# Attention by one batch at a time, two neighbouring chunks in step, with two tokens to a partition

## The chip, the cores and the metric

The kernel runs on one core of a Trainium2 chip. The core has a tensor engine (PE, with its weight loads shown apart as PEld), a vector engine (DVE), a scalar engine (ACT), GpSimd (POOL), a queue engine (SP) that issues most transfers, and 16 DMA engines that carry them. The metric is the device time of one execution in microseconds (us), as the median of the runs.

## The reference

Two blocks follow each other. The first is a causal linear attention with a decay per head, for 4 batches, 8 heads, 768 tokens and head width 64:

```
intra = (q_b k_b^T * Dmask) v_b          # Dmask[i, j] = lam^(i-j) for i >= j, else 0
inter = (q_b * lam^(i+1)) kv_state
out   = intra + inter
kv_state = lam^block * kv_state + (k_b * lam^(block-1-j))^T v_b
```

Its result, x of 4 x 768 x 512, goes into a Fourier mixing block with an MLP:

```
u  = x + real(fft(fft(x, over tokens), over channels))
un = (u - mean(u)) / sqrt(var(u) + 1e-6)
y  = u + relu(un @ w_ch1) @ w_ch2        # 512 -> 2048 -> 512
```

q, k, v are fp32; the two weight matrices arrive as 64-bit floats and are converted on the chip.

## The kernel before

**Attention.** The recurrence may be cut into chunks of any length; the kernel uses chunks of C = 128 tokens, so NC = 6 a batch. `attention` (L476 on) walks through 12 steps. A step handles the same chunk of two batches: batches 0 and 1 for the first six steps, 2 and 3 for the last six. `Side` (L309) holds the buffers of one of the two; the second side borrows room in the second halves of w1 and w2, which therefore can't be loaded before attention ends. For each side a step has these parts:

- `load`: k, q and v of a chunk, 128 tokens on 128 partitions, 256 KB each, in runs of the 64 floats that one head has for one token (L331, issued by SP, one step ahead).
- `turn_k`, `turn_q`: four transposes each on PE (L349, L357), read out of PSUM by ACT (L351, L359). POOL makes kd, k times its decay (L347). DVE makes qs, q times its decay (L363).
- `scores`: k times q for each head, 64 rows by 128 columns of the array (L370). DVE multiplies the result by the decay mask (L376).
- `from_state`: qs times the running state, 64 rows by 64 columns (L385), into the output bank po.
- `to_state`: kd times v, 128 rows by 64 columns (L392). POOL scales the old state (L398) and DVE adds (L399).
- `within`: v times the masked scores, 128 rows by 64 columns (L403), on top of po. ACT copies po out (L407).
- `back`: four transposes to tokens on partitions (L416), read out by ACT (L423 to L427), and, for batches 1 to 3, stored to DRAM. Batch 0 is kept on the chip with a mirrored copy.

In PE's order a step is scores, from_state, to_state, within, then the turns of the next step, then back.

**What follows attention.** `fft_ln(b)` folds a batch on DVE (`fold_x`, L541 to L545, and the lines after L609), transforms it by products with cosine and sine tables (L662, L674 to L679), normalises it and turns the result for the MLP (L693 to L727). `mlp` multiplies by w1 (L808) and w2 (L822). Its first three groups are done in halves of the hidden width, so that the first half can run before the second half of the weights is on the chip. Everything after that (from L900 on) is a Strassen-like scheme for the later groups, which the change doesn't touch.

**Weights.** `load_weights` (L202) brings a 512 KB piece of 64-bit floats (L215) and turns it into fp32 with two ACT and five DVE instructions (L226 to L236). There are 32 pieces. The first 16 use four raw buffers of the pool hp, the last 16 those of the pool ld that attention's loads used.

**Order.** Each of these is a generator that yields a cost; `mixed` (L1430) interleaves several by their shares of the cost. A scheduler then orders each engine's instructions by priority and hands out buffers as they come free; `keep_in_program_order` and `lead` pin some of them. The shares that matter stand at L1442 to L1458: five attention steps with a sixth of the weights; then attention with `fft_ln(0)` (`mix`); then the first half of the MLP (`lead_half`) with what is left of attention and of the first 16 pieces; then `lead_half` with `fft_ln(1)`, `fft_ln(2)` (`fr`) and the second 16 pieces. PSUM has eight banks: five in the pool pa, three in pm. While the flag `early` is set, attention takes from both; later pm is the MLP's and attention has pa alone.

Of the kernel before, what the change touches and what calls it, by code (L numbers as in the profile page):

```python
# [77 lines left out]
def kernel(  # L78
# [44 lines left out]
    ld = front_pool("ld", 2)  # L123
# [35 lines left out]
    decay = const.tile([C, H, C], F32, name="decay")  # L159
    for h in range(H):  # L160
        scan(decay[:, h, :], lamb[:, h:h + 1].broadcast_to([C, C]), ident, 0.0, op0=ALU.mult, op1=ALU.add)
# [8 lines left out]
    kpow = decay[:, :, C - 1:C].broadcast_to([C, H, D])  # L170
# [6 lines left out]
    turns_a = [const.tile([128, HP, D], F32, name=n) for n in ("st", "sd")]  # L177
# [24 lines left out]
    def load_weights(dst, src):  # L202
# [5 lines left out]
        if landed[0] < NW // 2:  # L208
            raw = hp_.tile([128, 2 * WP], U32, tag="hr", name=f"raw{cnt[0]}")
        else:  # L210
            raw = ld.tile([128, 3 * WP], U32, tag="kqv", name=f"raw{cnt[0]}")[:, 0:2 * WP]
# [72 lines left out]
    def pair(t, hp):  # L284
        return t[:, 2 * hp:2 * hp + 2, :].rearrange("p a d -> p (a d)")

    oTs, eo = {}, {}
    TWOS = ((0, 1), (2, 3))
    TURNED = (0,)
    first = const.tile([128, HP, 1], F32, name="first")  # L290

    spare = [w2[:, FO // 2 + i, :] for i in range(FO // 2)]
    spare += [w1[:, c, DFF // 2 + DM * i:DFF // 2 + DM * (i + 1)] for c in range(KO) for i in range(2)]
    turns_b = [spare[0][:, i * HP * D:(i + 1) * HP * D].rearrange("p (h d) -> p h d", h=HP) for i in range(2)]
    place = {n: spare[1 + i] for i, n in enumerate(
        ("k0", "k1", "q0", "q1", "v0", "v1", "kd", "kT", "qT", "qs", "oT", "sc0", "sc1"))}
# [11 lines left out]

    class Side:  # L309

        def __init__(self, b):
            self.b, self.two = b, b % 2
            self.turns = turns_b if self.two else turns_a
            self.kqv, self.now, self.next = {}, {}, {}

        def tile(self, shape, name, i=None):
            if self.two:
                t = place[name if i is None else f"{name}{i % 2}"]
                return t.rearrange("p (h d) -> p h d", h=shape[1])
            return new(at, shape, name, **({"bufs": 2} if name == "sc" else {}))  # L320

        def load(self, c):
            rows = slice(c * C, (c + 1) * C)
            if self.two:
                ts = [self.tile([C, H, D], n, c) for n in "kqv"]
            else:
                t = new(ld, [C, 3, H, D], "kqv")
                ts = [t[:, i] for i in range(3)]
            self.kqv[c] = ts
            for t, src in zip(ts, (k, q, v)):  # L330
                nc.sync.dma_start(t, src[self.b, :, rows, :].rearrange("h p d -> p h d"))  # L331
                yield 0.0

    sides = [Side(b) for b in range(B)]

    def lead(products):

        for i, mm in enumerate(products):
            if i == 0:
                tc.keep_in_program_order(mm)  # L340

    def turn_k(s, c):
        kt, qt, vt = s.kqv[c]
        s.next = n = {"vt": vt}
        if c < NC - 1:
            n["kd"] = s.tile([C, H, D], "kd")
            nc.gpsimd.tensor_tensor(n["kd"], kt, kpow, op=ALU.mult)  # L347
        pt = psum_t([128, HP, C])
        lead(nc.tensor.transpose(pt[:, hp, :], pair(kt, hp), ident) for hp in range(HP))  # L349
        n["kT"] = s.tile([128, HP, C], "kT")  # L350
        nc.scalar.copy(n["kT"], pt)  # L351
# [1057 lines left out]
    def run(gen):  # L1409
        return sum(gen)  # L1410
# [98 lines left out]
```

## Time and profile before

| | us |
|---|---|
| median of 3 runs | 775.61 (775.11 to 776.37) |
| the profiled execution | 773.71 |
| its span, first to last instruction | 771.9 |
| PE busy / PEld / DVE / ACT / POOL | 736.4 / 638.5 / 606.0 / 222.1 / 176.8 |
| mean granted PE clock | 0.992 of full speed |
| bytes moved | 123.36 MB in 156,651 packets, 114,478 of them under 512 B |

A profile's page gives busy times and shares, the span in 40 slices of 19.3 us (digits are tenths), the DMA queues, the chain of work that ended last, and the costliest groups of instructions. A group's line has the source line, engine, operation, output and input tiles, shapes and count, then its busy time, the mean of one in ns, and the idle time before it with what ended that. PE's instructions overlap, so a row's duration there is a latency; the distance between starts is the price. The time outside the span is 1.8 us.

### The profile page before, as it was taken

What the parts mean: (1) busy time and instruction counts of PE and PEld (TensorE: products, weight loads), DVE (VectorE), ACT (ScalarE), POOL (GpSimd) and SP (SyncE); (2) the same over time, 40 slices, a digit from 0 to 9 for tenths busy, and PEclk for the clock granted to TensorE, in tenths of its full rate; (3) what the DMA queues carried; (4) which work ended last, traced back from release to release, by engine and by line L of the source; (5) the groups of instructions that cost most, each with busy time, mean ns of one, the idle gap of its engine ahead of it and who ended that gap; (6) DMA issues with size and microseconds to landing.
All of it is one profiled execution on the core that took longest, in us unless ns stands there. A gap on an engine that the chain in (4) does not pass through costs nothing.

```text
span 771.9 us, 14917 instructions
## 1 busy us (share of the span) xinstructions
PE 736.4 (95%) x5784; PEld 638.5 (83%) x5784; DVE 606.0 (78%) x1167; ACT 222.1 (29%) x512; POOL 176.8 (23%) x200
## 2 busy tenths in 40 slices
PE   6898798998999999999899999999999999999997
PEld 5787697866586676759647899999999999999997
DVE  5988968778967488357965999788986699758984
ACT  4665444644341111002001221034301341024310
POOL 4422232210001124101105951360015001230013
PEclk9999998999999999999999999999999999999999
DMA  9999995455333346511441465876546455455542
GB/s 195 237 244 241 261 231 167 147 182 188 111 128 83 78 151 179 131 68 59 86 102 68 151 219 160 277 233 200 183 124 177 127 180 186 126 176 180 145 141 69
DMA packets 156651, 123.36 MB, mean 160 GB/s; under 512 B 114478, under 2 KB 117166, under 8 KB 156582
## 3 DMA queue, kind: packets, MB, share of 16 engines
q1 hardware_dynamic: 149232, 103.13, 48.9%
q0 software_dynamic: 4032, 12.99, 4.7%
q10 hardware_dynamic: 3318, 6.30, 2.3%
q8 instruction: 46, 0.75, 0.4%
q14 instruction: 23, 0.19, 0.1%
HBM read 90.66 MB, written 31.73 MB: 159 GB/s over the span
## 4 chain that ended last, share of the span: by engine, by line
PE 66%; DVE 14%; DMA 9%; issue 4%; SPq 3%; ACT 2%; POOL 1%; ACTq 0%; DVEq 0%; POOLq 0%
PE p L1257 19%; PE p L1183 17%; PE pm L808 8%; PE pm L822 7%; PE p L1090 6%; DMA raw<-in_moe_w_ch_dram 5%; PE pa L662 4%; SPq L331 3%; DMA w<-in_q_dram 2%; DVE w L236 1%; PE pa L370 1%; DMA ur<-utd 1%; DVE e L227 1%; ACT e L229 1%; DVE w L233 1%
## 5 line engine op out<-in xcount | busy, mean ns | idle before, releaser
L808 PE MATMUL pm<-ut,w 128*128 128x256 f32 x512 | 116.9, 381 | 5.9 <-ACT hr L816 3.3
L808 PEld LDWEIGHTS pm<-ut,w 128*128 128x128 f32 x512 | 95.5, 190 | 23.7 <-ACT hr L816 4.5
L822 PE MATMUL pm<-w,hr 128*128 128x512 f32 x240 | 104.9, 593 | 0.0
L822 PEld LDWEIGHTS pm<-w,hr 128*128 128x128 f32 x240 | 45.2, 190 | 52.6 <-issue 51.6
L1278 POOL TENSOR_TENSOR y<-y,u 128x512 f32<-128x512 f32 x12 | 19.9, 1661 | 186.8 <-DVE y L1287 100.4
L1257 PE MATMUL p<-tx,sx 128*128 128x128 f32 x400 | 52.7, 275 | 0.0
L1257 PEld LDWEIGHTS p<-tx,sx 128*128 128x128 f32 x400 | 48.6, 192 | 0.0
L1192 DVE TENSOR_TENSOR ha<-p,ha 128x512 f32<-128x512 f32 x60 | 40.0, 683 | 8.3 <-PE p L1183 8.1
L816 ACT ACTIVATE hr<-pm 128x256 f32<-128x256 f32 x44 | 16.6, 381 | 92.2 <-PE pm L808 91.8
L1263 ACT COPY y<-p 128x128 f32<-128x128 f32 x48 | 12.8, 266 | 103.6 <-PE p L1257 103.1
L1265 DVE TENSOR_TENSOR y<-p,y 128x128 f32<-128x128 f32 x92 | 25.4, 283 | 15.9 <-PE p L1257 9.3
L1257 PE MATMUL p<-w,ha 128*128 128x128 f32 x288 | 37.4, 275 | 0.0
L1192 DVE TENSOR_TENSOR hs<-p,hs 128x512 f32<-128x512 f32 x39 | 26.1, 683 | 12.3 <-PE p L1183 12.3
L1257 PEld LDWEIGHTS p<-w,ha 128*128 128x128 f32 x288 | 34.9, 192 | 0.1
L1183 PE MATMUL p<-sx,tx 128*128 128x128 f32 x264 | 33.9, 275 | 0.0
L226 ACT ACTIVATE e<-raw 128x512 bf16<-128x512 int16 x32 | 21.9, 683 | 37.7 <-DMA raw<-in_moe_w_ch_dram 33.7
L1183 PEld LDWEIGHTS p<-sx,tx 128*128 128x128 f32 x264 | 31.6, 192 | 0.0
L797 POOL DMA_INDIRECT out_dram<-y,ix x12 | 13.5, 1127 | 75.8 <-DVE y L857 64.1
L229 ACT ACTIVATE e<-e,cvt 128x512 uint16<-128x512 uint16 x32 | 22.9, 717 | 26.3 <-DVE e L227 24.5
L1183 PE MATMUL p<-ur,w 128*128 128x128 f32 x216 | 28.0, 275 | 0.0
L1190 ACT COPY ha<-p 128x512 f32<-128x512 f32 x24 | 14.0, 584 | 48.3 <-PE p L1183 48.3
L347 POOL TENSOR_TENSOR kd<-kqv,decay 128x512 f32<-128x512 f32 x10 | 11.2, 1120 | 70.3 <-DMA kqv<-in_k_dram 26.6
(355 smaller groups left out, 1805.3 us busy)
## 6 DMA issues: line engine op xcount, KB each, us to landing
tx<-td SPq DMA_DIRECT2D x84, 256.0 KB, 2.9
raw<-in_moe_w_ch_dram SPq DMA_DIRECT2D x32, 512.0 KB, 4.2
tx<-sd SPq DMA_DIRECT2D x63, 256.0 KB, 2.8
td<-tx SPq DMA_DIRECT2D x21, 256.0 KB, 2.0
ud<-x SPq DMA_DIRECT2D x16, 256.0 KB, 2.4
utd<-e SPq DMA_DIRECT2D x64, 64.0 KB, 2.7
u<-ud SPq DMA_DIRECT2D x16, 256.0 KB, 4.1
kqv<-in_k_dram SPq DMA_DIRECT2D x12, 256.0 KB, 5.9
```

Of the source, the lines that this page charges most:

```text
L226: pin(nc.scalar.activation(sg, top.bitcast(I16), AF.Sign))
L229: nc.scalar.activation(pw, pw, AF.Relu, bias=cvt[:, 0:1], scale=8.0)
L331: nc.sync.dma_start(t, src[self.b, :, rows, :].rearrange("h p d -> p h d"))
L662: mm = nc.tensor.matmul(ps[:, n, :], lhsT=piece(a, i, n), rhs=cs[0:rows, a, i in (2, 3), n, :], start=(a == 0), stop=(a == 1))
L808: nc.tensor.matmul(ps, lhsT=w1[:, c, 128 * fc:128 * fc + 128], rhs=ut[:, c, :], start=(c == 0), stop=(c == KO - 1))
L822: return nc.tensor.matmul(ps, lhsT=hr[(fc - f0) // 4][:, fc % 4, 128 * i:128 * i + 128], rhs=w2[:, fc, :], start=(fc == f0), stop=(fc == f ...
L1090: nc.tensor.matmul(ps, lhsT=s2.A[a][:, kt, 128 * i:128 * i + 128], rhs=U[b][:, kt, :], start=(first and kt == 0), stop=(kt == 1), skip_gro ...
L1183: nc.tensor.matmul(ps[:, 128 * i:128 * i + 128], lhsT=ab[m][0][:, 128 * i:128 * i + 128], rhs=ab[m][1], start=(start and i == 0), stop=Tru ...
L1192: V.tensor_tensor(o, p, o, op=ADD)
L1257: nc.tensor.matmul(ps[:, 0:HM // 2], lhsT=ab[m][0][i], rhs=ab[m][1][:, i, :], start=(start and i == 0), stop=(i == HF // 2 - 1), skip_grou ...
L1265: V.tensor_tensor(o, ps[:, 0:HM // 2], o, op=ADD)
L1278: nc.gpsimd.tensor_tensor(o, y, u, op=ADD)
```

## The change

Attention goes through one batch after the other. A superstep `i` handles two neighbouring chunks of one batch, 256 tokens, so there are three supersteps a batch and 12 in all.

- `load`: partition p holds tokens 2p and 2p + 1, so a run is 128 floats (512 B) and a load is 512 KB. Partitions 0 to 63 then hold the first chunk and 64 to 127 the second; even and odd tokens lie side by side (index r).
- `apart` copies k and q so that even and odd tokens stand apart, with POOL (the first superstep with ACT), and makes kd from the uncopied k.
- `turn_k`, `turn_q` transpose even and odd tokens one after the other; the copies of q write every second column.
- `scores`, `from_state`, `to_state` and `within` use 64 rows by 64 columns throughout: row half and column half are given by the chunk and the head's parity. There are twice as many products of half the size, in an order that names the four quarters in turn.
- Three states in turn instead of two a side; the state goes through both chunks of a superstep one after the other.
- The order of a superstep in PE's program is the turns of i + 1, back of i - 1, to_state of i + 1, within of i, then from_state and scores of i + 1.
- The pool ld has three buffers of 4 KB a partition instead of two of 6 KB; k, q and the copied k share them, and the second 16 weight pieces use them later. The borrowed rooms in w1 and w2 are laid out anew.
- The tables are loaded at supersteps 1 and 2. The shares at the end are set anew: attention with three weight units until batch 0 is done, then `mix` with attention and the weights, then 13 units of `lead_half` with 2.4 t_step of attention and what is left of the first 16 pieces, then 24 units of it with attention's rest, then `fr` and the second 16 pieces.

```diff
-    ld = front_pool("ld", 2)
+    ld = front_pool("ld", 3)
...
+    def load(i, names):
+        b, n = divmod(i, SC)
+        for name in names:
+            t = kqv[i, name] = v_of[i % 2] if name == "v" else new(ld, [128, H, 2, D], "kqv")
+            src = {"k": k, "q": q, "v": v}[name]
+            nc.sync.dma_start(t.rearrange("p h r d -> p h (r d)"),
+                              src[b, :, 2 * C * n:2 * C * (n + 1), :].rearrange("h (p r) d -> p h (r d)", r=2))
...
+    def apart(i, copy=nc.gpsimd.tensor_copy):
+
+        kt, qt = kqv[i, "k"], kqv[i, "q"]
+        for name, t in (("k2", new(ld, [128, 2 * DM], "kqv")), ("q2", q2)):
+            t = kqv[i, name] = t.rearrange("p (r x) -> p r x", r=2)
+            copy(t.rearrange("p r (h d) -> p r h d", h=H), kqv.pop((i, name[0])).rearrange("p h r d -> p r h d"))
+        w = decay[:, :, C:C - 2:-1].rearrange("p h (r o) -> p h r o", o=1).broadcast_to([128, H, 2, D])
+        nc.gpsimd.tensor_tensor(kd, kt, w, op=ALU.mult)
...
+    def to_state(i):
+        n, vt = i % SC, kqv[i, "v"]
+        chunks = (0, 1) if n < SC - 1 else (0,)
+        pu = [psum_t([128, HP, D]) for _ in chunks]
+        lead(mm(pu[ch][HD[hi], hp, :], lhsT=kd[HD[ch], 2 * hp + hi, r, :], rhs=vt[HD[ch], 2 * hp + hi, r, :],
+                start=(hp + r == 0), stop=(r == 1), skip_group_check=True)
+             for hp in range(HP) for r in range(2) for ch in chunks for hi in range(2))
...
+    def scores(i):
+        pss = [[psum_t([128, HP, C]) for _ in range(2)] for _ in range(2)]
+        lead(mm(pss[hi][r][HD[ch], hp, :], lhsT=kT[HD[hi], r, hp, D * ch:D * ch + D], rhs=qT[HD[hi], hp, C * ch:C * ch + C],
+                start=True, stop=True)
+             for r in range(2) for hp in range(HP) for ch in range(2) for hi in range(2))
...
+    def crossed(i, ch):
+        return int(ch == 1 and i // SC not in TURNED)
...
+        for i in range(n):
+            if i + 1 < n:
+                turn_k(i + 1)
+                turn_q(i + 1)
+                yield 2.2
+            if i:
+                yield from back(i - 1)
+            if i + 1 < n:
+                to_state(i + 1)
+                yield 1.4
+            within(i)
+            yield 2.0
+            if i + 2 < n:
+                load(i + 2, "v")
+            if i in TABLES:
+                load_tables(TABLES[i])
+            if i + 1 < n:
+                yield from begin(i + 1)
+            if i + 2 < n:
+                apart(i + 2)
+            if i + 3 < n:
+                load(i + 3, "kq")
...
-    run(mixed((att, 5 * t_step), (w, 0.16 * NW)))
-    run(mixed((att, t_step), (mix, 4.4), (w, 1.0)))
-    run(mixed((att, 2.0 * t_step), (mix, T_FOLD - 4.4), (w, 1.0)))
-    run(mixed((att, 2.0 * t_step), (mix, 24.0), (w, 2.0)))
+    run(mixed((until(att, lambda: (0, 0) in xs), 40.0), (w, 3.0)))
+    run(mixed((mix, T_FOLD), (att, 1.8 * t_step), (w, 1.0)))
+    run(mixed((mix, 24.0), (att, 2.5 * t_step), (w, 4.0)))
     run(mix)
     early[0] = False
...
-    run(mixed((lead_half, 24.0), (att, 2.0 * t_step), (w, NW / 2 - 9.0)))
-    run(mixed((att, 99.0), (w, NW / 2 - landed[0])))
-    run(mixed((lead_half, t_half - 24.0), (fr, 62.0), (w, 0.5 * NW)))
+    run(mixed((lead_half, 13.0), (att, 2.4 * t_step), (w, NW / 2 - landed[0] - 0.4)))
+    run(mixed((lead_half, 24.0), (att, 99.0)))
+    run(att)
+    run(mixed((lead_half, t_half - 37.0), (fr, 62.0), (w, 0.5 * NW)))
```

More of the change, by code (lines that the diff above doesn't have):

```diff
@@ L307 @@
     early = [True]
[L309 to L332, printed above, removed]
@@ L334 @@
-    sides = [Side(b) for b in range(B)]
+    kqv, po = {}, {}
+    mm = nc.tensor.matmul
     def lead(products):
-        for i, mm in enumerate(products):
+        for i, m in enumerate(products):
             if i == 0:
[L340 to L351, printed above, removed]
@@ L1417, in part, with until @@
                 return
+    def until(gen, reached):
+        while not reached():
+            yield next(gen)
     def chain(gens):
```

250 lines of the change are left out of this document (123 added, 127 removed).

## The prediction

> **What bounds the kernel now.** I read the page's shares and 40 slices first, then the busy times by stage, the chain in order of time, the waits, and last the single instructions of attention. On the page:
>
> ```profile
> PE 736.4 (95%) x5784; PEld 638.5 (83%) x5784; DVE 606.0 (78%) x1167; ACT 222.1 (29%) x512; POOL 176.8 (23%) x200
> PE   6898798998999999999899999999999999999997
> DVE  5988968778967488357965999788986699758984
> DMA  9999995455333346511441465876546455455542
> PE 66%; DVE 14%; DMA 9%; issue 4%; SPq 3%; ACT 2%; POOL 1%; ACTq 0%; DVEq 0%; POOLq 0%
> ```
>
> Over the whole span PE is the bound (771.9 - 736.4 = 35.5 us idle). In the first six slices, where attention runs, it isn't: the transfer engines are full. Busy time by stage (PE, PEld, DVE, ACT, POOL, then granted clock, DMA share, GB/s):
>
> ```profile
> 0.00:20.00 20.00, 13.56 (x168) 11.54 (x168) 10.38 (x22) 8.12 (x16) 8.29 (x20) 1.00 1.01 202
> 0.00:47.00 47.00, 37.70 (x585) 33.06 (x586) 35.66 (x63) 25.28 (x55) 20.49 (x32) 1.00 1.05 222
> 47.00:118.00 71.00, 61.69 (x902) 56.03 (x903) 58.68 (x109) 36.95 (x90) 17.18 (x17) 0.98 1.01 246
> 118.00:151.00 33.00, 29.46 (x264) 26.04 (x263) 24.76 (x58) 16.55 (x38) 10.27 (x10) 0.90 0.48 148
> 151.00:240.00 89.00, 85.62 (x414) 58.97 (x413) 73.89 (x164) 39.61 (x84) 5.17 (x6) 1.00 0.43 138
> ```
>
> To 118 us DMA is at 100%, PE idles 118 - 99.4 = 18.6 us (6.4 of them in the first 20 us) and DVE is busy 94.3. From 118 to 151 PE idles 3.5 us more and the clock is 0.90, worth another 33 x 0.10 = 3.3. From 151 to 240 PE idles 3.4 us in 89. The chain shows why the early steps are slow:
>
> ```profile
> 31.01 6.07 DMA w<-in_q_dram
> 40.25 0.89 PE pa L370 x16
> 60.57 6.66 DMA w<-in_q_dram
> 92.90 1.32 PE pa L370 x16
> 108.65 9.11 DMA raw<-in_moe_w_ch_dram
> ```
>
> A q load or a weight load of 6 to 9 us recurs in it. Five attention steps lie between the scores at 40.25 and 92.90, so one takes 10.5 us.
>
> **The loads.** 18.9 MB of k, q and v (72 loads of 256 KB) come in runs of 64 floats (256 B); the change makes 36 loads of 512 KB in runs of 512 B. The last part of this kernel has loads with 512 B runs (the utd blocks). A window with only the one kind, then one with only the other:
>
> ```profile
> DMA packets 9720, 2.46 MB, mean 224 GB/s; under 512 B 9719, under 2 KB 9719, under 8 KB 9719
> DMA packets 904, 0.45 MB, mean 300 GB/s; under 512 B 24, under 2 KB 904, under 8 KB 904
> kqv<-in_k_dram SPq DMA_DIRECT2D x12, 256.0 KB, 5.9
> ```
>
> Both windows are full. 18.9 MB take 84 us at 224 GB/s and 63 at 300: 21 us of transfer time leave the first 118. If the new loads ran no faster than 224 GB/s, the term would be 0, its near end. What remains, 97 us, is less than PE's 99.4 + 6.4, so DMA no longer sets this stage. Of the 18.6 - 6.4 = 12.2 us that PE idles behind loads I take 9 back (ends 0 and 12.2), since DVE stands close behind at 94.3 of 118. In 118 to 151 PE waited for batch 0's normalisation, and cooled; batch 0 now finishes after three supersteps instead of six steps, with seven supersteps left to lie beside its transform. I take 3 of the 6.8 us (0 to 6.8). Sum: **-12** (0 to -19).
>
> The Trainium skill, page "DMA: Bandwidth & Descriptors", section "Specifications", gives 512 B as the least size for line rate, about 27 GiB/s an engine. By it 16 engines would bring 18.9 MB in about 41 us (an estimate from that page); the 300 GB/s above disagrees. With 41 us the term would lean to its far end, not beyond it, since only PE's idle time can be won.
>
> **PE's own work.** A superstep has the tokens of a step of now (256). In rows:
>
> ```profile
> 60.21 0.27 PE L370 MATMUL pm<-w 64*128 64x128 f32 x1
> 60.32 0.27 PE L370 MATMUL pm<-w 64*128 64x128 f32 x1
> 60.52 0.32 PE L385 MATMUL pa<-qs,st 64*64 64x128 f32 x1
> 60.91 0.27 PE L385 MATMUL pa<-w,w 64*64 64x128 f32 x1
> 61.02 0.27 PE L385 MATMUL pa<-w,w 64*64 64x128 f32 x1
> 83.74 0.69 PE L392 MATMUL pa<-kqv,kd 128*64 128x64 f32 x16
> 84.26 0.64 PE L392 MATMUL pa<-w 128*64 128x64 f32 x16
> 84.72 1.05 PE L403 MATMUL pa<-sc,kqv 128*64 128x128 f32 x16
> 85.60 1.04 PE L403 MATMUL pm<-w,w 128*64 128x128 f32 x16
> 87.07 0.60 PE L349 MATMUL pa<-ident,w 128*128 128x128 f32 x4
> 87.50 0.60 PE L357 MATMUL pa<-ident,kqv 128*128 128x128 f32 x4
> ```
>
> Scores go two at a time, a pair per 0.11 us: 32 instructions, 1.7 us a step. State products (L385) already go in four quarters, four per 0.11 us. New scores are 64 instructions, 16 fours, again 1.7. L403 takes 0.88 per 16, 1.76 a step; new, 16 fours, 1.7. L392 takes 0.52 per 16, 1.04 a step; new 0.9 to 1.04. Transposes stay at 6 x 0.43 = 2.6. PE per superstep: 2.6 + 1.7 + 1.04 + 0.86 + 1.7 = 7.9 to 8.1 us, as now; quarters save nothing in streaming. Each change of form costs 0.20 - 0.11 = 0.09 (60.32 to 60.52); four a step become two: 12 x 2 x 0.09 = **-2** (0 to -4). In batch 0, whose rows aren't crossed, the state products use two of the four quarters: 0.86 more in two supersteps and some in the first, **+1** (0 to 2).
>
> **The start.**
>
> ```profile
> L359 ACT COPY qT<-pa 128x512 f32<-128x512 f32 x9 | 5.4, 600 | 0.8 <-PE pa L357 0.8
> ```
>
> k and q of the first superstep are 512 KB each and are copied apart on ACT before the first transpose (a 512-wide copy takes 0.60, so at most 1.2 us for 1024); the halves of a second batch drop out. kd is twice as wide on POOL. **+2** (0 to 4).
>
> **The copies on POOL.** Two 128x1024 copies a superstep are new (apart); kd and the state's scaling stay. Rows by form:
>
> ```profile
> L347 POOL TENSOR_TENSOR kd<-kqv,decay 128x512 f32<-128x512 f32 x10 | 11.2, 1120 | 70.3 <-DMA kqv<-in_k_dram 26.6 <-PE pa L392 14.9 <-PE pm L392 14.5
> L398 POOL TENSOR_TENSOR sd<-st,qpow 128x256 f32<-128x256 f32 x4 | 3.1, 777 | 0.0
> L529 POOL MEMSET ys<- 128x386 f32 x5 | 1.9, 412 | 0.0
> L227 DVE TENSOR_SCALAR e<-raw 128x512 uint16<-128x512 uint16 x21 | 10.7, 508 | 10.1 <-DMA raw<-in_moe_w_ch_dram 10.1
> ```
>
> And three rows in order of time:
>
> ```profile
> 63.31 1.15 POOL L347 TENSOR_TENSOR kd<-kqv,decay 128x512 f32<-128x512 f32 x1 [16.32 <-DMA kqv<-in_k_dram]
> 63.46 1.28 DVE L227 TENSOR_SCALAR e<-raw 128x512 uint16<-128x512 uint16 x1
> 97.83 0.41 DVE L227 TENSOR_SCALAR e<-raw 128x512 uint16<-128x512 uint16 x1
> ```
>
> A POOL copy of this size isn't in the trace. By the memset, which only writes (412 ns for 386), 1024 columns take 1.1 us; by the product with two inputs (1120 for 512) 2.2. A copy has one input; I take 1.4. POOL per superstep: 2 x 1.4 + 2.2 + 2 x 0.78 = 6.6 us, against 2 x 1.12 + 2 x 0.78 = 3.8 now, so 12 x 2.8 = 34 us more. The rows in order of time show the price on DVE: a weight step that takes 0.41 alone began 0.15 us after POOL did, took 1.28 and ended 0.28 after it. Over 21 pieces its mean is 508, so about 2 us of such waiting; with five steps a piece, 10 us beside the 37.7 us that POOL worked up to 118. 34 us more make +9 on DVE in proportion (ends 0 and 15). Most of that lies in DVE's idle time (24 of 118): **+3** on the path (0 to 12). If that cover is gone, all 9 to 15.
>
> **The tail of attention.** The first MLP products of now, and the span of the within products:
>
> ```profile
> 130.56 1.89 PE L808 MATMUL pm<-ut,w 128*128 128x256 f32 x8
> L403 PE MATMUL pa<-w,w x128: 272/273/323, 13.0 to 166.0; 128*64 128x128 f32 x128
> ```
>
> The second half of the weights still needs attention's buffers and so its end, and more of the MLP (37 of the schedule's units against 24) is spent before it. In 151 to 240 DVE is 83% busy, mostly converting these weights. Less filler beside the same DVE work lets PE run dry: +3 (0 to 10). A third raw buffer in that stage (the pool has three of 4 KB a partition, not two of 6) works against it, -1 (0 to -4). Together **+2**. The PSUM banks belong here too: with the early rotation off, two of five banks are held from one superstep to the next, so scores wait for DVE's masks more often; the MLP beside them is the cover, and its loss is within the 10.
>
> SP issues 36 loads for 72, so it costs nothing; but a k load waits for POOL's kd to free its buffer, and the weight loads queue behind it. Their cover is the four raw buffers.
>
> **Sum** on the profiled execution, 773.7 us (span 771.9 and 1.8 around it): 773.7 - 12 - 2 + 1 + 2 + 3 + 2 = 767.7. The median of the runs shown is 1.9 above the profiled one, so **769.6**, 0.8% faster.
>
> **Rivals.** *POOL takes over as the pace (slower).* The three buffers for k, q and the copied k make a ring: kd(i), load of k(i+1), copy of k, copy of q, kd(i+1).
>
> ```profile
> xn<-xa SPq DMA_DIRECT2D x4, 256.0 KB, 2.8
> ```
>
> With a load that lands as in this row (2.8, and 0.9 for the second 256 KB at 300 GB/s) and my copy it is 3.7 + 1.4 + 1.4 + 2.2 = 8.7 us. With one that lands as today's, 5.9, and a copy of 1.7 it is 11.5. It decides from 10.5, today's step, on. Then nothing of the 12 comes back; batch 0's four supersteps and the four beside its transform lose 1.0 each, DVE's waiting lies inside that, and the rest stays: 773.7 + 8 - 2 + 1 + 2 + 2 = 784.7, median **787**. For it speaks the 1.28 us row, against it that fewer, longer runs should shorten the landing. The Trainium skill, page "SBUF — State Buffer", section "Who interferes with whom", says that GpSimd and some DVE instructions take a shared port for a whole instruction while the other blocks fully; the 1.28 us row agrees. It would make a 1024-wide instruction hold DVE up to twice as long as today's, which adds to this case's chance.
>
> *Given back later.* For it speaks DVE's 83% there, against it the third raw buffer. The 12 us are won by 150 us, but the weights' second half lands no earlier since DVE sets 151 to 240; PE waits there instead (+9 instead of +2): 774.7, median **777**, about no change.
>
> *All of it.* Copies are cheap, PE is never short: 773.7 - 19 - 4 + 0 + 2 + 0 - 2 = 750.7, median **753**. PE's 35.5 us allow it; DVE's 94.3 of 118 speaks against it.
>
> *Quarters don't run together* as written: pairs instead of fours for scores, within and to_state add 12 x 4.4 = 53 us, **825**; the L385 rows speak against it.
>
> **Chances.** Forecast (763 to 773) 0.42; all or most of the gain (below 763) 0.15; given back (773 to 779) 0.16; POOL (above 779) 0.25; quarters 0.02. The forecast's own range is 763 to 774; 8 in 10 needs 755 to 788. A measurement of this kernel tells about 0.2% from no change (774.1 to 777.2 are the same): faster 0.60, same 0.12, slower 0.28.
>
> **What would show it.** Loads: DMA share under 1 between 40 and 110 us, and packets under 512 B down by 18.9 MB / 256 B, some 73,000. PE: scores, within and to_state in fours per 0.11 us. Earlier batch 0: the first L808 before 115 us instead of 130.6. POOL: the copies' duration; waits of the transposes for POOL, and DVE's weight steps over 1 us, mean the slower rival. Tail: PE idle of more than 10 us between attention's last product and 250 us means the gain was given back. I am wrong in kind if PE's idle time to 151 us doesn't fall from 22 us.

## The result and the profile after

The changed kernel takes **815.98 us** as the median of 4 runs (815.61 to 820.46), the kernel before 775.36 us beside it (773.0 to 776.37): a ratio of 1.0542, 95% interval 1.0498 to 1.0585. The medians lie 40.6 us apart (the means 42.0); 769.6 us was forecast. The profiled execution has a span of 814.3 us (771.9 before), so it carries the loss.

The page of the changed kernel: busy times and shares; the slices of PE, of the granted clock and of DMA; packets; shares of the chain.

```profile
PE 756.0 (93%) x6872; PEld 657.1 (81%) x6872; DVE 612.6 (75%) x1173; ACT 225.6 (28%) x512; POOL 195.9 (24%) x215
PE   4796777969999998999999999999999999999997
PEclk9798998988999998999999999999999999999999
DMA  9764645461345244742143236667554556455442
DMA packets 119220, 123.50 MB, mean 152 GB/s; under 512 B 40174, under 2 KB 79726, under 8 KB 119142
PE 73%; DVE 14%; DMA 6%; POOL 3%; issue 2%; ACT 1%; SPq 0%; DVEq 0%; ACTq 0%; POOLq 0%
```

The transfers did become lighter: packets under 512 B fell by 74,304 and DMA's slices, which were 9 in a row for six slices, stand at 9, 7, 6, 4, 6, 4. But PE idles 814.3 - 756.0 = 58.3 us instead of 35.5, and its slices of 4, 7, 6, 7 and, but for one 8, the clock's of 7 and 8 lie in the first ten, 204 us. The loss is 42.4 us of span: 22.8 are idle time. The mean clock fell from 0.992 to 0.972, which is worth at most 814.3 x 0.028 - 771.9 x 0.008 = 16.6 us. Part of the slow clock falls into PE's idle time and costs nothing. Read in steps of 0.1 us, the trace has PE busy at half clock for 33.6 us instead of 8.8; half of the difference, 12.4 us, is the price (four of the within products start every 0.21 us there and every 0.11 at full clock). The other 7 us are busy time of PE that neither explains; they stay unplaced.

Busy time by stage of the changed kernel (PE, PEld, DVE, ACT, POOL, then clock, DMA share, GB/s):

```profile
0.00:20.00 20.00, 9.51 (x172) 8.10 (x172) 9.22 (x22) 6.59 (x9) 10.06 (x21) 1.00 0.90 259
0.00:118.00 118.00, 86.80 (x1855) 79.60 (x1855) 78.83 (x144) 51.46 (x113) 47.44 (x54) 0.91 0.64 187
118.00:151.00 33.00, 24.86 (x358) 21.85 (x359) 29.40 (x57) 15.39 (x35) 11.50 (x13) 0.90 0.51 163
151.00:206.00 55.00, 47.04 (x750) 38.32 (x750) 33.22 (x61) 23.59 (x50) 8.69 (x9) 0.91 0.47 148
206.00:240.00 34.00, 34.00 (x126) 21.84 (x121) 20.00 (x48) 11.83 (x25) 1.90 (x2) 1.00 0.42 132
```

To 118 us DMA is at 0.64 and yet PE idles 31.2 us where it idled 18.6, and runs at 0.91 of its clock. To 151 us it idles 31.2 + 8.1 = 39.3 instead of 22. From 206 to 240 us, where attention has ended, it doesn't idle at all. Nearly the whole loss is made by then: the last products of attention and the first of the late part, by instruction, after and then before:

```profile
L405 PE MATMUL pa<-w,w x256: 269/269/418, 26.2 to 205.9; 64*64 64x128 f32 x128
L1191 PE MATMUL p<-ur,w x216: 275/275/275, 543.9 to 750.2; 128*128 128x128 f32 x108
```

```profile
L1183 PE MATMUL p<-ur,w x216: 275/275/275, 501.7 to 707.9; 128*128 128x128 f32 x108
```

Attention ends at 205.9 instead of 166.0 us, 39.9 later; the late part starts 42.2 later. What PE waits for up to attention's end (us in total, times, longest; the 7.4 is the wait before the first product):

```profile
PE pa L356 <- DVE w L390: 9.7, 2, 5.2
PE pm L349 <- ACT kqv L341: 7.4, 1, 7.4
PE pa L384 <- DVE w L390: 4.5, 1, 4.5
PE pm L356 <- DVE w L390: 3.8, 1, 3.8
PE pa L356 <- DVE sc L390: 3.4, 1, 3.4
PE pa L369 <- DMA w<-in_v_dram: 2.7, 2, 2.3
PE pm L349 <- DVE st L380: 2.3, 1, 2.3
```

16.9 us stand between `turn_q` (L356) and the masks (L390), 4.5 more between the scores (L384) and the masks. `turn_q` reads nothing that the masks write. What it needs from them is a PSUM bank: the two output banks of `from_state`, the four of the scores and the two of `turn_k` are all eight. One such place in order of time (start, duration, what ended the wait):

```profile
66.90 0.66 PE L349 MATMUL pm<-ident,kqv 128*128 128x128 f32 x4
67.39 0.60 PE L349 MATMUL pa<-ident,kqv 128*128 128x128 f32 x4
71.46 0.20 ACT L619 COPY fe<-fe 128x2 f32<-128x2 f32 x1 [6.95 <-DVE fe L552]
71.56 0.58 ACT L350 COPY w<-pm 128x512 f32<-128x512 f32 x1
72.03 0.42 DVE L624 TENSOR_TENSOR fe<-fe 128x257 f32<-128x257 f32 x1
72.36 0.68 DVE L390 TENSOR_TENSOR w<-pa,decay 128x512 f32<-128x512 f32 x1
73.19 1.09 PE L356 MATMUL pa<-ident,w 128*128 128x128 f32 x4 [5.21 <-DVE w L390]
```

The scores are done at 67; DVE has batch 0's folds in its order first and comes to the mask at 72.36; PE stands from 67.99 to 73.19. In the old order from_state and to_state, some 2 us, and within lay between the scores and the next turns; now turn_k alone does, 1.1 us. In this place ACT is late too: it reads the turned k (L350) out of its two banks only from 71.56 on, behind a copy (L619) that waits for the same folds. No run changed the order of ACT by itself.

Such a wait can be paid twice. Four stretches of the changed kernel (columns as above):

```profile
31.67:35.09 3.42, 3.42 (x57) 3.25 (x50) 2.61 (x5) 1.79 (x4) 1.32 (x2) 1.00 1.04 318
35.09:38.50 3.41, 1.06 (x29) 0.85 (x29) 1.83 (x4) 3.15 (x8) 0.70 (x1) 1.00 0.40 103
38.50:41.91 3.41, 3.41 (x74) 3.41 (x73) 2.69 (x3) 0.00 (x0) 1.92 (x1) 0.50 0.23 68
69.22:76.05 6.83, 2.85 (x13) 2.65 (x14) 6.83 (x15) 2.43 (x5) 0.85 (x2) 0.50 0.01 2
```

PE stood for 2.35 us from 35.39 on, and then ran for 3.41 us at half clock; around the wait of 5.21 us the half clock lasted 6.83. From the first product to the last, half clock comes in stretches of 3.41 us or a multiple, two in the kernel before and eight in the changed one. In the 3.41 us ahead of each, PE was busy for less than half of the time: 1.3 and 1.4 us before, 0.5 to 1.65 us after. On the same grid no stretch at full clock with more than 1.7 us of work was followed by one in the two kernels. The boundary isn't exact: in chain_masks_banks and mf_banks_copies one drop each came after 2.5 and 2.0 us of work.

### The profile page after: what moved, and what is told of

Read it like the earlier page. It is cut to its first block, busy times and chain, and to the rows that moved or that the text cites. A ratio compares the mean times of both kernels' runs of the same rounds, so it can differ in the third digit from the quotient of the medians.

```text
span 814.3 us, 17075 instructions
## 1 busy us (share of the span) xinstructions
PE 756.0 (93%) x6872; PEld 657.1 (81%) x6872; DVE 612.6 (75%) x1173; ACT 225.6 (28%) x512; POOL 195.9 (24%) x215
## 4 chain that ended last, share of the span: by engine, by line
PE 73%; DVE 14%; DMA 6%; POOL 3%; issue 2%; ACT 1%; SPq 0%; DVEq 0%; ACTq 0%; POOLq 0%
PE p L1265 20%; PE p L1191 16%; PE pm L830 10%; PE pm L816 9%; PE p L1098 5%; PE pa L670 4%; DMA raw<-in_moe_w_ch_dram 2%; PE pa L384 1%; PE pa L405 1%; DVE un L722 1%; DVE e L230 1%; DMA w<-in_v_dram 1%; DVE w L236 1%; DMA x<-xb,ix 1%; DVE stt L701 1%
## 5 line engine op out<-in xcount | busy, mean ns | idle before, releaser
L1265 PEld LDWEIGHTS p<-tx,sx 128*128 128x128 f32 x400 | 48.7, 192 | 0.0
L384 PE MATMUL pa<-w 64*64 64x128 f32 x608 | 28.8, 284 | 11.1 <-DVE w L390 4.5
L1273 DVE TENSOR_TENSOR y<-p,y 128x128 f32<-128x128 f32 x92 | 25.5, 285 | 16.3 <-PE p L1265 9.3
L1200 DVE TENSOR_TENSOR hs<-p,hs 128x512 f32<-128x512 f32 x39 | 26.2, 685 | 12.3 <-PE p L1191 12.3
L384 PEld LDWEIGHTS pa<-w 64*64 64x64 f32 x608 | 24.6, 139 | 12.6 <-DVE w L390 5.0
L343 POOL TENSOR_TENSOR w<-kqv,decay 128x1024 f32<-128x1024 f32 x12 | 23.6, 1968 | 32.2 <-PE pa L369 22.5
```

The lines of the kernel that those rows point to most:

```text
L343: nc.gpsimd.tensor_tensor(kd, kt, w, op=ALU.mult)
L384: lead(mm(pss[hi][r][HD[ch], hp, :], lhsT=kT[HD[hi], r, hp, D * ch:D * ch + D], rhs=qT[HD[hi], hp, C * ch:C * ch + C], start=True, stop=Tr ...
L1200: V.tensor_tensor(o, p, o, op=ADD)
L1265: nc.tensor.matmul(ps[:, 0:HM // 2], lhsT=ab[m][0][i], rhs=ab[m][1][:, i, :], start=(start and i == 0), stop=(i == HF // 2 - 1), skip_grou ...
L1273: V.tensor_tensor(o, ps[:, 0:HM // 2], o, op=ADD)
```

## The experiments

All are edits of the changed kernel, but for one of the kernel before. No edit drops or alters part of the computation. A time is the median of its runs; the ratio is to the kernel before, run beside it.

| run | us (range) | ratio, 95% interval | PE idle | clock |
|---|---|---|---|---|
| changed kernel | 815.98 (815.61 to 820.46) | 1.0542 (1.0498 to 1.0585) | 58.3 | 0.972 |
| loads_256 | 816.08 (815.35 to 817.08) | 1.0521 (1.0462 to 1.0581) | 54.9 | 0.970 |
| folds_spread | 811.45 (806.33 to 812.95) | 1.0471 (1.0412 to 1.0530) | 53.7 | 0.976 |
| masks_first | 810.13 (808.20 to 816.41) | 1.0493 (1.0422 to 1.0565) | 48.8 | 0.981 |
| copies_act | 809.87 (808.71 to 812.41) | 1.0465 (1.0425 to 1.0506) | 54.2 | 0.977 |
| state_dve | 813.59 (812.95 to 815.59) | 1.0513 (1.0475 to 1.0550) | 59.1 | 0.976 |
| banks_long | 806.57 (805.54 to 808.53) | 1.0416 (1.0377 to 1.0455) | 52.3 | 0.973 |
| all_four | 810.96 (807.45 to 815.54) | 1.0478 (1.0420 to 1.0536) | 58.6 | 0.976 |
| mf_banks_copies | 803.01 (800.25 to 803.69) | 1.0368 (1.0307 to 1.0429) | 48.7 | 0.980 |
| chain_masks_banks | 803.82 (801.75 to 804.67) | 1.0399 (1.0370 to 1.0429) | 45.4 | 0.980 |
| no_copies | 823.54 (820.34 to 824.34) | 1.0606 (1.0571 to 1.0641) | 46.4 | 0.981 |
| no_copies_kd2 | 825.69 (823.09 to 829.85) | 1.0642 (1.0590 to 1.0693) | 47.2 | 0.975 |
| nc_kd2_folds | 815.48 (813.30 to 819.51) | 1.0531 (1.0490 to 1.0572) | 41.5 | 0.984 |

Only banks_long, mf_banks_copies and chain_masks_banks have intervals clear of the changed kernel's on the fast side, and no_copies_kd2 on the slow side; the other differences are read together with their traces.

**Are the larger pieces worth anything?**

```diff
+            x = src[b, :, 2 * C * n:2 * C * (n + 1), :].rearrange("h (p r) d -> p h r d", r=2)
+            for r in range(2):
+                nc.sync.dma_start(t[:, :, r, :], x[:, :, r, :])
```

> The changed kernel with each load of q, k and v made as two, one for each of the two tokens of a partition, so that the pieces are 256 bytes again and the rest is unchanged. If the larger pieces are worth what the prediction gave them, about 12 us, this kernel takes 825 to 830 us. If the loads are off the path of the changed kernel, because attention is held by VectorE and the banks, it stays within 2 us of the changed kernel's 816 us.

Packets and stage of this run:

```profile
DMA packets 156660, 123.50 MB, mean 152 GB/s; under 512 B 114478, under 2 KB 117166, under 8 KB 156582
0.00:118.00 118.00, 89.57 (x1862) 83.22 (x1862) 76.80 (x142) 52.64 (x113) 46.90 (x53) 0.91 0.79 185
```

The packets are back at the old count and DMA's share to 118 us is 0.79 instead of 0.64, but the time is the same. The pieces are worth nothing here: over the first 118 us DMA isn't full in either, because attention itself has become slower than its loads. What larger pieces would bring to the old order, where DMA is full, wasn't tried.

**Attention by itself.** In these runs all supersteps are recorded ahead of weights, folds and norms; only the stretch of attention is compared, one profiled execution each. In the kernel before the same is done, with six units of weights beside the folds instead of four.

```diff
+    run(att)
+    run(mixed((mix, T_FOLD), (w, 4.0)))
+    run(mixed((mix, 24.0), (w, 4.0)))
```

> The changed kernel with its stages in another order: all 12 supersteps of attention are recorded first, with no weight step, fold or norm among them (those follow, so the whole is not comparable in time; only the stretch of attention is read). Theory A, the masks stand in VectorE's queue behind folds, weight steps and norms, and TensorE stops because its eight PSUM banks hold unread scores: without that company a superstep takes about what TensorE itself needs, 8 to 9.5 us, so the last product of attention ends near 110 to 120 us (205.9 us in the changed kernel) and TensorE idles under 10 us between 15 us and there. Theory B, the chain of single buffers (one kd, one q2, one k2 at a time, through GpSimd and the load ring) sets the pace: 11.5 us or more a superstep even alone, the last product near 145 us or later, with TensorE waiting on GpSimd or on the loads in every superstep.

> The same for the kernel before: all 12 supersteps first, weight steps and folds after. Theory A: its attention alone is no slower or faster than the new one by more than 10 us, since both ask the same 8 us of TensorE a superstep; the last product near 105 to 120 us. Theory B: the old form, with two buffers of most things, runs its supersteps at about 9 us where the new one takes 11.5 or more, so it ends at least 25 us sooner than the new one.

The within products, new form (start of the first to start of the last), and what PE waited for most in it up to 145 us:

```profile
L405 PE MATMUL pa<-w,w x240: 269/269/472, 23.4 to 143.8; 64*64 64x128 f32 x120
PE pa L369 <- DMA w<-in_v_dram: 8.2, 3, 3.4
```

The same line of the old form, and its stretch from 20 to 121 us:

```profile
L403 PE MATMUL pm<-w,w x80: 272/273/273, 31.9 to 121.7; 128*64 128x128 f32 x80
20.00:121.00 101.00, 92.22 (x1532) 84.59 (x1530) 46.43 (x81) 49.36 (x118) 24.76 (x30) 0.97 0.97 238
```

Even without company the new form ends 22 us later, (143.8 - 23.4) / 11 = 10.9 us a superstep; the old one goes at (121.7 - 13.8) / 11 = 9.8 with DMA at 0.97. The last product at 143.8 us, and 22 us of difference, both lie between what the two theories gave. The whole programs took 819.49 and 792.02 us (one run each). So masks behind company can't be all. Theory B, the loading chain through POOL, was the next to be tried.

**The loading chain without copies.** A product with the identity turns one head's 64 columns out of the loaded tile.

```diff
-            lead(nc.tensor.transpose(pt[:, hp, :], k2[:, r, 128 * hp:128 * hp + 128], ident) for hp in range(HP))
+            lead(mm(pt[HD[hi], hp, :], lhsT=kt[:, 2 * hp + hi, r, :], rhs=ident, start=True, stop=True)
+                 for hp in range(HP) for hi in range(2))
```

> The changed kernel without the step that sets the two tokens of a partition apart: each turning product takes one head (64 columns) instead of two as it stands in the loaded tile and is turned by a product with the identity, so the two GpSimd copies of 1.05 us, the third tile of the load ring and q2 fall away; kd stays single. Theory B (the chain from kd over the load of k, the copies and back to kd sets 10.8 us a superstep, which the run with attention alone showed against 9.2 us of TensorE): about 1.5 us a superstep come back and the start gets 1 to 2 us earlier, 798 to 806 us. Theory A (masks behind other work on VectorE decide when there is company): TensorE waits for masks instead, 811 to 817 us.

> As the run without the copies, and kd gets a second buffer where q2 was, so that nothing in the loading chain is single any more. Theory B: another 0 to 6 us faster than without the copies alone. Theory A: the same as without the copies within 3 us.

> Attention recorded alone first, as before, now without the copies and with two kd. Theory B: the superstep falls from 10.8 us to TensorE's own 9.2 to 9.6 us, and the last product of attention ends at 118 to 126 us instead of 144.0, as in the old form (121.9). If it stays above 138 us, it is neither the copies nor kd nor the ring, but the order itself (the states' additions, the masks, the two banks of the output).

> Without the copies, two kd, and the folds of batch 0 spread over 3.0 units of attention. If the two causes are separate, their gains add: the folds' 4.5 us on top of what the run without copies and with two kd gains. If a masks' wait only takes the place of the chain's, the two together gain no more than the larger of them.

The turns of k into pa in the run without copies, and then in the changed kernel:

```profile
L346 PE MATMUL pa<-ident,kqv 128*64 128x128 f32 x256 | 18.9, 299 | 2.0 <-ACT oT L410 1.1 <-issue 0.7 <-DVE w L389 0.2
```

```profile
L349 PE MATMUL pa<-ident,kqv 128*128 128x128 f32 x64 | 10.4, 299 | 0.8 <-DVE w L390 0.4 <-POOL kqv L341 0.3
```

The price of the edit hid its gain. Turning by products costs 18.9 us for 256 instructions (two to a product), where 64 transposes of the same data cost 10.4. Over the run PE is busy 775.6 us instead of 756.0, 19.6 more, and the time rose by 7.6: PE's idle time fell from 58.3 to 46.4 us, so about 12 us came back. A second kd gave nothing. The alone run, with no copies and two kd, has its last within product at 158.1 us (833.23 us for the whole, one run). By its expectation that speaks against the chain, but its turns are dearer, so it decides nothing. Spreading the folds on top of no_copies_kd2 gains 10 us, with intervals that don't meet, more than on its own below. That what the chain held back, masks behind folds hold back next, would fit; it isn't shown.

**Copies and states off POOL, and more banks.**

```diff
-                apart(i + 2)
+                apart(i + 2, nc.scalar.copy)
...
-                    nc.gpsimd.tensor_tensor(s_new, s_old, spow.broadcast_to([128, HP, D]), op=ALU.mult)
+                    nc.vector.tensor_tensor(s_new, s_old, spow.broadcast_to([128, HP, D]), op=ALU.mult)
...
     run(mix)
-    early[0] = False
...
     run(att)
+    early[0] = False
...
-    run(mixed((mix, T_FOLD), (att, 1.8 * t_step), (w, 1.0)))
-    run(mixed((mix, 24.0), (att, 2.5 * t_step), (w, 4.0)))
+    run(mixed((mix, T_FOLD), (att, 3.0 * t_step), (w, 2.0)))
+    run(mixed((mix, 24.0), (att, 2.0 * t_step), (w, 3.0)))
```

The four edits are, in this order, copies_act, state_dve, banks_long and folds_spread; all_four has them together.

> The changed kernel with the two copies that set the tokens apart on ScalarE in every superstep (it was GpSimd in all but the first), so that GpSimd has only kd and the states' scaling left. TensorE's work is unchanged. Theory B (the loading chain through GpSimd): the queue ahead of kd and of the scaling gets 2.1 us a superstep shorter; half of what the run without copies gave back beside its dearer products (it asked some 22 us more of TensorE and took 7 to 8 us more) comes through, 803 to 811 us. Theory A: within 3 us of 816 us.

> The changed kernel with the states' scaling on VectorE instead of GpSimd. The new order runs two chunks of one batch in a superstep, so two scalings and two additions stand in series between to_state and the next from_state, with two passes from GpSimd to VectorE and back, where the old order had one of each for two independent batches. Theory C (this series is on the path): 1 to 2 us of every superstep come back, 800 to 810 us, although VectorE gets about 10 us more work. Theory A (VectorE is what is short): slower, 817 to 822 us.

> The changed kernel with attention drawing on all eight PSUM banks until its end, instead of on five from the first product of the mlp on. Theory D (from there the two output banks and the four of the scores don't fit into five, so that the scores wait for masks in the middle: 0.6, 2.2, 0.9, 2.1 and 4.5 us between 138 and 183 us): 5 to 10 us come back, 806 to 811 us. If only VectorE's lateness counts and not the number of banks, the waits move to the turning products and the time stays within 3 us of 816.

> The changed kernel with other shares: batch 0's folds are spread over 3.0 units of attention instead of 1.8, as thinly as in the kernel before, with the weight steps that fall due in that time. Theory A: the two waits of TensorE at 68 and 85 us (5.2 and 4.5 us, behind folds on VectorE) fall below 3 us together, and the kernel takes 806 to 812 us. Theory B, or PSUM banks short whatever VectorE does: waits of the same length stay, and the time is within 2 us of 816.

> Four edits of the changed kernel together: copies on ScalarE, scaling on VectorE, eight banks to the end of attention, the folds over 3.0 units. If the causes are separate, the gains of the single runs add (the folds' was 4.5 us) and the kernel takes 785 to 800 us; if all of them relieve one and the same shortage, it gains no more than the largest of them by itself, 803 to 812 us. To beat the kernel before it would have to fall below 774 us, which none of the theories gives.

The copies on ACT bring 6 us, with intervals that overlap. A part of that may be DVE's own time:

```profile
PE 753.0 (93%) x6872; PEld 654.9 (81%) x6872; DVE 604.8 (75%) x1173; ACT 245.1 (30%) x534; POOL 173.0 (21%) x193
```

DVE did the same 1173 instructions in 604.8 us instead of 612.6: 7.8 us less while POOL copies nothing. These are single executions, and the sum also moves with the order: folds_spread, with the copies on POOL, has 605.8. The states on VectorE bring 2.4 us, inside the intervals. Eight banks to the end bring 9.4 us, the largest single gain, and the scores' wait for masks is gone from the list, while `turn_q`'s grew (21.3 instead of 16.9 us):

```profile
PE pa L356 <- DVE w L390: 10.9, 3, 5.7
PE pm L356 <- DVE w L390: 7.8, 2, 5.2
PE pa L356 <- DVE sc L390: 2.6, 1, 2.6
```

The folds, spread, gain 4.5 us, but waits of 5.2 and 4.5 us only gave way to others of up to 6.4 us, for masks again, and the next `turn_k` (L349), which hardly waited for masks in the changed kernel (0.4 us), now does. Its row in folds_spread:

```profile
PE pa L349 <- DVE w L390: 6.9, 2, 6.3
```

And the four together gain only 5 us, less than the banks alone, though the two intervals overlap. That they relieve, in part, the same thing would fit; which of them costs something beside the others isn't shown.

**Masks ahead of company.** Each DVE instruction of the weight steps and of batch 0's transform is tied behind the attention instructions recorded before it.

```diff
+        for i in new_:
+            if i.engine == dve:
+                if prev is not None:
+                    tc.add_manual_dep(i, prev.name, mybir.DependencyInfo(mybir.DependencyClass.NoSync, mybir.DependencyReason.DATA), reason="behind")
+                prev = i
...
+            d = (next(p[0], None) if p[0] is not w and p[0] is not mix else company(p[0])) if p[2] < p[1] else None
```

> The changed kernel in which every VectorE instruction of batch 0's folds, norms and of the weight steps is ordered behind those attention instructions that were recorded before it; so the masks of two supersteps move ahead of 5 to 10 fold instructions in VectorE's queue, and nothing else is changed. Theory A (masks behind company): TensorE's waits of 5.2 and 4.5 us for masks at 68 and 85 us vanish, and the kernel takes 803 to 809 us. Rival: the folds only come that much later and the norms and the first mlp product with them, so the time stays within 3 us of 816 us.

> The changed kernel with masks ahead of company, eight banks to the end of attention, and copies on ScalarE. If the causes add once the masks don't wait behind company: 7 to 10 us by the masks, 9 by the banks and 6 by the copies, so 790 to 797 us. If they relieve the same shortage: 803 to 808 us.

PE's waits in masks_first:

```profile
PE pa L356 <- DVE w L390: 6.4, 2, 5.0
PE pa L356 <- DVE sc L390: 2.6, 1, 2.6
```

`turn_q` waits 9.0 us for masks instead of 16.9, PE idles 48.8 instead of 58.3, the clock is 0.981, and the time is 5.9 us shorter (the intervals overlap). With the banks and the copies on top, the excess over the kernel before falls from 5.4% to 3.7%, 13 us; the single gains would have been 21. ACT's copies and the banks were not taken out of this run one by one.

**What attention by itself lacks.** Copies on ACT, states on DVE and a third buffer for v, loaded with k and q:

```diff
+    v_of.append(flat(new(hp_, [128, 2, DM], "hr")))
...
-            t = kqv[i, name] = v_of[i % 2] if name == "v" else new(ld, [128, H, 2, D], "kqv")
+            t = kqv[i, name] = v_of[i % 3] if name == "v" else new(ld, [128, H, 2, D], "kqv")
...
-                load(i + 2, "v")
...
-                load(i + 3, "kq")
+                load(i + 3, "kqv")
```

> Attention recorded alone first, with copies on ScalarE, the states' scaling on VectorE and three buffers for v instead of two, loaded with k and q; TensorE's work is that of the changed kernel. If the loading chain, the states' series and the two buffers of v are what attention by itself loses, the superstep falls from 11.4 us (144.0 less 20 us over 11) to 9.2 to 9.8 us and the last product ends at 120 to 128 us, as in the old form (121.9). If it ends above 135 us, something else in the new order is slow, such as the turning of the scores' banks.

> Attention recorded alone first with three buffers of v, copies and states on GpSimd as in the changed kernel. If the two buffers of v were the cause (9.5 us of TensorE's waits name v's loads), the last product ends at 128 to 135 us; if the copies and the states on GpSimd set the pace, it stays at 138 to 144 us.

> Attention recorded alone first with copies on ScalarE and states on VectorE, but two buffers of v. If GpSimd's queue was the cause, the last product ends at 126 to 132 us; if the two buffers of v were, it stays at 136 to 144 us with TensorE waiting for v's loads.

The last within products with the third buffer only:

```profile
L406 PE MATMUL pa<-w,hr x80: 269/269/320, 46.1 to 128.4; 64*64 64x128 f32 x80
```

And PE's waits with the other two edits only:

```profile
PE pa L369 <- DMA w<-in_v_dram: 9.6, 3, 4.7
PE pm L369 <- DMA w<-in_v_dram: 7.2, 3, 3.4
```

All three edits: last within product at 126.5 us, 801.07 us for the whole program. The third buffer alone: 128.4, and 801.26 us for the whole program, 18 less than 819.49. The other two without it: 150.3 and 823.98 us. So it is v (one execution each, but the times lie far apart). `to_state(i + 2)` reads v a superstep ahead of `within(i + 2)`, so v is held for two supersteps and two buffers leave the load of v(i + 2) no time but that from within(i) to to_state(i + 2). In the new form alone:

```profile
92.42 1.43 SPq L330 DMA_DIRECT2D w<-in_v_dram  x1
100.18 1.12 PE L369 MATMUL pa<-w 64*64 64x64 f32 x16 [2.87 <-DMA w<-in_v_dram]
```

The load goes out at 92.42, right behind within (which ended at 91.55), PE has 6 us of other work and stands 2.87 us. Theory B fell with this: neither the copies nor the states nor the ring of k set attention's own pace.

**All of it in company.**

> The changed kernel with all that helped: copies on ScalarE, states on VectorE, three buffers of v, masks ahead of folds, norms and weight steps, eight banks to the end of attention. If the loading chain is short in company too, it gains on the run with masks, banks and copies (803 us): 788 to 797 us. If in company VectorE is what is short, the states' scaling there costs as much as the chain gives back: 800 to 806 us. Faster than the kernel before (774 us) by neither.

803.82 us: the third buffer and the states on DVE add nothing to mf_banks_copies. With company a superstep takes (205.9 - 26.2) / 11 = 16.3 us in the changed kernel (a step of the old one (166.0 - 13.0) / 11 = 13.9), and there the load of v has time enough (2.7 us of waits). The third buffer of v also takes one of the four raw buffers of the weights in this run, which may cost something; that wasn't tried apart. The waits that are left:

```profile
PE pa L357 <- DVE w L391: 6.6, 3, 3.6
PE pa L726 <- DVE un L721: 3.5, 2, 3.2
PE pm L385 <- ACT oT L412: 3.3, 2, 2.1
```

So attention first, with three buffers of v (801.26 and 801.07 us, one run each), is about as fast as the best version in company. No version beats the kernel before.

## Why the prediction was wrong

**The loads (-12): wrong, measured 0.** The mechanism came as described: DMA's share under 1 from 20 us on, 74,304 fewer small packets (73,000 forecast), a full DMA no longer in the way. The step that failed is "Of the 18.6 - 6.4 = 12.2 us that PE idles behind loads I take 9 back". It took the waits behind loads as idle time that simply falls away, and weighed only DVE's total of 94.3 us against it. What came in its place was a wait that the old kernel hardly had: PE idles 31.2 us to 118 us instead of 18.6, and masks, not loads, lead its list of waits. Undoing the larger pieces moved nothing (816.08 against 815.98). The other 3 of the 12 failed as well: from 118 to 151 us PE idles 8.1 us instead of 3.5, at the same clock of 0.90.

**The tail and the banks (+2): the term that was mis-sized most.** The prediction named the mechanism, "two of five banks are held from one superstep to the next, so scores wait for DVE's masks more often", gave it no term of its own, put its loss "within the 10" of another and thought of it for the tail only. Eight banks to the end of attention gave 9.4 us back. And waits of PE for masks begin at 20 us, with all eight banks in use: 16.9 us before `turn_q`. The new order of a superstep was known, but the prediction didn't count banks along it (2 + 4 + 2 of 8 before `turn_q`), nor ask what lies between the scores and the next need of a bank. Less filler beside the weights, the reason that it did give for the tail, didn't matter: PE idles 0 us from 206 to 240.

**The clock: a missing term.** It cost 12.4 us by the trace's half-clock stretches, 16.6 at most by the means. The prediction counted the old clock's loss as something to win and never priced a colder one. 2.35 us without work were enough for half clock, where PE had only 1.06 us of work in the 3.41 us from 35.09 on. The Trainium skill, page "TensorE: Matmul & The Clock Gate", section "Part 1: The HAM clock gate", puts the fall to half clock at an idle window of about 3.4 us. The stretches of 3.41 and 6.83 us agree with the window's length, but the windows ahead of them weren't idle, only less than half filled. Section "Part 4: PE-mode transpose" of the same page of the Trainium skill says that a transpose doesn't count as busy in the same way. The trace doesn't bear that out here: from 31.67 to 35.09 us PE was busy throughout, 2.5 us of it with transposes, and full clock followed.

**PE's own work (-2, +1): not borne out.** Scores, within and to_state go in fours, as forecast. But PE's busy time rose by 19.6 us, of which the clock explains 12.4. In attention alone, up to the last within product (144 and 122 us) and with work at half clock counted at half, PE is busy 107.3 us in the new form and 104.9 in the old, 2 more where 1 less was forecast. Whether the changes of form gained their 2 us can't be read from this.

**The start (+2): right in kind, too small.** The first transpose comes at 7.4 us instead of 5.1, as forecast. But by 20 us PE has worked 9.51 us instead of 13.56, 4 less, since the turns of the second superstep wait too: 2.3 us for a bank that a state's addition frees, and right after 20 us 3.4 for masks that stand behind a weight step on DVE.

**The copies on POOL (+3): the mechanism right, the size about twice that.** A copy took 1.10 us in the mean, the near end, where I took 1.4. One beside the folds shows the price on DVE:

```profile
L341 POOL COPY w<-kqv 128x1024 f32<-128x1024 f32 x11 | 12.1, 1099 | 16.0 <-PE pm L356 10.8 <-PE pa L356 5.2
66.31 0.41 DVE L552 TENSOR_TENSOR fe<-fe 128x255 f32<-128x255 f32 x1
68.11 1.17 POOL L341 COPY kqv<-kqv 128x1024 f32<-128x1024 f32 x1 [2.27 <-issue]
68.30 1.25 DVE L552 TENSOR_TENSOR fe<-fe 65x255 f32<-65x255 f32 x1
```

A fold of this width takes 0.41 us alone; this one took 1.25 and ended 0.27 us after the copy. DVE's busy time was 7.8 us lower without the copies (+9 forecast), and the time 6 us, both with the reservations above.

**The rivals.** POOL as the pace (787) fell as a mechanism: with copies and states off POOL attention alone was no faster. That the time falls into its class all the same, above 779 with a chance of 0.25, is luck. A ring of buffers did set attention's own pace, but it was v's, which the prediction didn't look at, and only without company. "Given back later" fell: nearly the whole loss is made by 206 us. Quarters did run together (for that rival, 53 us on top of the forecast would be 822, not 825). The sign that the prediction set for being wrong in kind came: PE's idle time to 151 us is 39.3 us, not under 22; and the first product with w1 comes at 135.1 us, not before 115.

**What stays open.** Of 42 us, the banks, the order of masks on DVE and the copies on POOL account for 13 together, shown by taking them away. With these, and the states and v besides, 30 us remain (803.82 against 773.97). In that run, 28.0 us longer in span, PE idles 9.9 us more than before and is busy at half clock for 26.0 us instead of 8.8, which costs 8.6; some 9 are unplaced. After the start, the remaining waits are again `turn_q` behind masks, a state, an output bank, and the normalised batch (L726), none over 3.6 us in company. That one batch in step, whose products hang on each other, leaves PE less that could run than two batches did, would fit. It isn't shown.

## What to carry to other kernels

A resource that is full is worth relieving only as far as the next chain reaches: before taking its waits as won, walk one round of the new order on the engine that is the bound and count the buffers and banks held at every point, and the engine that must free each. When a step is moved ahead of another that reads the same data, that data is held longer; count its buffers again. And price new waits in the matrix engine with the slow clock behind them: here it came where less than about half of a 3.41 us stretch was filled.

## What the hardware showed unexpectedly

- Half clock came after a wait of only 2.35 us. It came in stretches of 3.41 us or a multiple, in both kernels after a stretch that PE had filled to less than half (0.5 to 1.65 us of work).
- Turning by products with the identity (two heads of 64 columns side by side) cost 18.9 us where transposes of the same data cost 10.4, both fp32 and with the half-clock stretches of the first 210 us in them.
- A fold of 0.41 us on DVE took 1.25 us beside a copy of 1.17 us on POOL that doesn't touch the same data.
- Pieces of 512 B instead of 256 B lowered DMA's share from 0.79 to 0.64 to 118 us for the same bytes.
